# A decode step of two attention and two MLP layers with its gradients: the weighted sums over the cache taken four blocks per matmul instead of two

## The chip, the cores and the metric

The kernel runs on one core of one Trainium2 chip. The metric is the device time of one execution in microseconds (us). Before the change the median of three runs is 1138.2 us (1136.74 to 1139.24). One execution was also recorded by the hardware profiler; its span is 1136.1 us, and every figure below that is not a run time comes from that recording. The engines are named as the profile names them: PE is the matmul engine, PEld its weight loads, DVE the vector engine, ACT the scalar engine, POOL the GpSimd engine, and SP the queue that issues most transfers.

## The reference

Two rounds of attention over a key and value cache and of an MLP, for a batch of two and one new token, and then the gradients of all inputs but one. Cut to what matters here:

```python
def _A_ref(x, k_cache, v_cache, wq, wo):            # Hq=32, Hkv=4, Sk=16384, Dh=128, B=2
    q = (x @ wq).reshape(B, Sq, Hq, Dh).transpose(0, 2, 1, 3)
    k = jnp.repeat(k_cache, rep, axis=1)            # rep = 8 query heads per cache head
    v = jnp.repeat(v_cache, rep, axis=1)
    p = _softmax(jnp.einsum("bhqd,bhkd->bhqk", q, k) * (Dh ** -0.5), axis=-1)
    o = jnp.einsum("bhqk,bhkd->bhqd", p, v)
    return o.transpose(0, 2, 1, 3).reshape(B, Sq, Hq * Dh) @ wo

x = x + _A_ref(_layernorm(x), k_cache, v_cache, wq, wo)     # layer 0
x = x + _B_ref(_layernorm(x), w1, b1, w2, b2)
x = x + _A_ref(_layernorm(x), k_cache, v_cache, wq, wo)     # layer 1, same caches and weights
x = x + _B_ref(_layernorm(x), w1, b1, w2, b2)
# outputs: x and the gradients of x, both caches and the weights (jax.vjp)
```

The change concerns two sums over the 16384 cache positions: the forward output `o = p V` of each layer, and in the backward pass `dq = dS K` of layer 0 (the same sum of layer 1 is left as it is). There are 8 groups (2 batch rows x 4 cache heads), each with 8 query heads. The cache of one group is 128 blocks of 128 positions x 128 features; it is read in four chunks of 32 blocks, 1 MB each.

## The kernel before

The sums are made by the class `Acc`. One call of `quad` handles half a chunk, 16 blocks. The coefficients of two neighbouring blocks (8 heads x 2 blocks = 16 columns) are the stationary operand; the two blocks side by side (256 wide) are the moving one. Four such matmuls in a row go to four column tiles of the array (`cg` = 0, 32, 64, 96), each with its own 16 partitions of the accumulator. The accumulators of two groups lie side by side in one PSUM bank, 256 columns each. Of the 16 x 256 results of a matmul half are wanted (each head with its own block); `reduce` picks them with the selector `sel2` and adds up the four tiles.

```python
sel2 = const.tile([128, 16], F32, name="sel2")     # folds the four 32-row tiles, 16 rows each
...
e_all = pers.tile([128, G, NP, 2, 8, 2], BF16, name="e_all")   # partition, group, pair of blocks, layer, head, block
...
class Acc:
    def __init__(self, g, src, coef, finish, half=0):
        ...
        self.acc = ACCT[:, half * 256:half * 256 + 256] if half < 2 else pm_([128, 256], F32, "acc2")[:]
        zero = lambda: V.memset(self.acc, 0.0)
        ...
    def quad(self, c, q, coef=None):
        ...
            self.cv = self.pre.pop(c) if c in self.pre else kv_load(self.src, self.g, c)
        for i in range(8):
            u = c * CP + q * 8 + i
            cg = 32 * (i % 4)
            t = 2 * (q * 8 + i)
            PE.matmul(self.acc[cg:cg + 16, :], lhsT=coef(u),
                      rhs=self.cv[:, t:t + 2, :].rearrange("p t d -> p (t d)"),
                      start=False, stop=True, tile_position=(0, cg), skip_group_check=True)
    def evac(self):
        self.sb = wrk.tile([128, 2, 128], F32, name="acc_sb")
        evac_cast(self.sb[:].rearrange("p a b -> p (a b)"), self.acc, 256)
        ...
    def reduce(self):
        ...
        for t in range(2):
            PE.matmul(ps, lhsT=self.sb[:, t, :], rhs=sel2v[:, t, :], start=(t == 0), stop=(t == 1))
        self.finish(ps)
```

The forward attention works in slots, 16 per group. Each slot turns 8 key blocks by PE transposes (`emit_T`, L420), has them copied out of PSUM by ACT or DVE, and makes the 8 score matmuls of two slots before (L573). After the last score of a group come its maximum (L508), the exponentials on ACT (L537), and the 8 quads (L452), which are laid between the slots of the next group:

```python
def attn_fwd(l, q_bf, rbc, oT, groups):
    ...
    def post(g):
        max_half(g, 1)
        ...
        a = Acc(g, "V", lambda u: e_all[:, g, u, l].rearrange("p h t -> p (h t)"), finish, g % 2)
        sch.later(2, p1)
        sch.later(4, p2)
        for i in range(16):
            sch.later(5 + i // 2, lambda i=i: ex(i // 8, i % 8))
        sch.later(9, lambda: queue_acc(sch, a, range(0, 2), False))
        sch.later(13, lambda: queue_acc(sch, a, range(2, 4), True))
        ...
    while s < len(slots) + 2 or sch.busy():
        ...
        kTs[s] = emit_T(cv, b, True)                          # 8 transposes
        sch.run_slot(1 if s < len(slots) else 2)              # maybe a quad
        if 2 <= s < len(slots) + 2:
            score(s - 2)                                      # 8 score matmuls
        s += 1
```

Chunks and weights are loaded into a pool of seven 1 MB buffers (`ld`, `NLD = 7`) by SP in program order, each load as soon as a buffer comes free; the chunks of the last group stay in buffers of their own for later use.

The last pass (from about 733 us to the end) computes the gradients of both layers' caches, reads both caches again and writes both gradients; its scheduler places two quads per chunk for layer 0's dq (`dq_quad`), with coefficients `dX`, which holds both layers in the same layout as `e_all`. Most of its PE results go through four PSUM banks (`xm`) that ACT and DVE empty by copies (L161, L164).

Of the kernel before, what the change touches and what calls it, by code (L numbers as in the profile page):

```python
# [10 lines left out]
F32 = mybir.dt.float32  # L11
I32 = mybir.dt.int32
# [11 lines left out]
def kernel(  # L24
# [78 lines left out]
    def pm_(shape, dtype, name):  # L103
        return ps_sm.tile(shape, dtype, name=name, tag="sm")
# [10 lines left out]
    V.memset(ones_bf[:], 1.0)  # L115
    neghalf = const.tile([128, 2], F32, name="neghalf")
    V.memset(neghalf[:], -0.5)
    sel2 = const.tile([128, 16], F32, name="sel2")
    V.tensor_tensor(out=sel2[:], in0=identf[:, 0:16], in1=identf[:, 32:48], op=ALU.add)
    V.tensor_tensor(out=sel2[:], in0=sel2[:], in1=identf[:, 64:80], op=ALU.add)  # L120
    V.tensor_tensor(out=sel2[:], in0=sel2[:], in1=identf[:, 96:112], op=ALU.add)
    sel2v = sel2[:].rearrange("p (h t) -> p t h", t=2)
    e_all = pers.tile([128, G, NP, 2, 8, 2], BF16, name="e_all")
    hot3 = const.tile([128, 128], BF16, name="hot3")
    m3 = const.tile([128, 1], F32, name="m3")
    V.tensor_reduce(out=m3[:], in_=identf[:, 64:128:32], axis=AX.X, op=ALU.add)
# [298 lines left out]
    class Acc:  # L425

        def __init__(self, g, src, coef, finish, half=0):
            self.g, self.src, self.coef, self.finish = g, src, coef, finish  # L430
            self.pre = {}
            self.cv = None
            self.acc = ACCT[:, half * 256:half * 256 + 256] if half < 2 else pm_([128, 256], F32, "acc2")[:]
            self.half = half
            zero = lambda: V.memset(self.acc, 0.0)
            if half in Acc.in_use:
                Acc.then[half] = zero
            else:
                zero()
            Acc.in_use.add(half)  # L440

        def quad(self, c, q, coef=None):
            coef = coef or self.coef
            if q == 0 and self.get is not None:
                self.cv = self.get(c)
            elif q == 0:
                self.cv = self.pre.pop(c) if c in self.pre else kv_load(self.src, self.g, c)
            for i in range(8):
                u = c * CP + q * 8 + i
                cg = 32 * (i % 4)  # L450
                t = 2 * (q * 8 + i)
                PE.matmul(self.acc[cg:cg + 16, :], lhsT=coef(u),  # L452
                          rhs=self.cv[:, t:t + 2, :].rearrange("p t d -> p (t d)"),
                          start=False, stop=True, tile_position=(0, cg), skip_group_check=True)

        def evac(self):
            self.sb = wrk.tile([128, 2, 128], F32, name="acc_sb")
            evac_cast(self.sb[:].rearrange("p a b -> p (a b)"), self.acc, 256)
            if self.half in Acc.then:
                Acc.then.pop(self.half)()  # L460
            else:
                Acc.in_use.remove(self.half)

        def reduce(self):
            ps = px([128, 8], F32, "o_ps")[:] if self.alloc is None else self.alloc()[:, 0:8]
            for t in range(2):
                PE.matmul(ps, lhsT=self.sb[:, t, :], rhs=sel2v[:, t, :], start=(t == 0), stop=(t == 1))
            self.finish(ps)

        alloc = get = None  # L470
# [30 lines left out]
    def attn_fwd(l, q_bf, rbc, oT, groups):  # L501
        sch = Sched()
        slots = [(g, c, b) for g in groups for c in range(NCH) for b in range(NB)]
        kTs, sc, st = {}, {}, {}

        def max_half(g, f):
            m = small.tile([128, 8], F32, name="mx%d" % f)
            V.tensor_reduce(out=m[:], in_=sc[g][f][:], axis=AX.X, op=ALU.max)  # L508
            charge("D", 0.7)
            st[g].append(m)  # L510

        def post(g):
            max_half(g, 1)
            m0, m1 = st[g]
            V.tensor_tensor(out=m0[:], in0=m0[:], in1=m1[:], op=ALU.max)
            esum = small.tile([128, 2, 8], F32, name="esum")
            negm = small.tile([128, 8], F32, name="negm")
            box = {}

            def p1():  # L520
                box["pm"] = pm_([8, 128], F32, "pm")
                PE.transpose(box["pm"][:, :], m0[:], identf[:])
                gm = small.tile([8, 1], F32, name="gm")
                V.reduce_max(out=gm[:], in_=box["pm"][:, :], axis=AX.X)
                box["dg"] = small.tile([8, 8], F32, name="dg")
                V.tensor_scalar(out=box["dg"][:], in0=identf[0:8, 0:8], scalar1=gm[:, 0:1], scalar2=None, op0=ALU.mult)
                charge("D", 0.5)

            def p2():
                pm2 = pm_([128, 8], F32, "pm2")  # L530
                PE.matmul(pm2[:], lhsT=onesf[0:8, :], rhs=box["dg"][:], start=True, stop=True)
                V.tensor_scalar(out=negm[:], in0=pm2[:], scalar1=-1.0, scalar2=None, op0=ALU.mult)  # L532
                charge("D", 0.2)

            def ex(f, h):
                half = NP // 2
                S.activation(out=e_all[:, g, f * half:(f + 1) * half, l, h, :],  # L537
                             in_=sc[g][f][:, h, :].rearrange("p (a b) -> p a b", b=2),
                             func=ACT.Exp, bias=negm[:, h:h + 1], scale=1.0, accum_out=esum[:, f, h:h + 1])
                charge("A", 0.3)  # L540

            def fin1():
                V.tensor_tensor(out=esum[:, 0, :], in0=esum[:, 0, :], in1=esum[:, 1, :], op=ALU.add)

            def fin2():
                pm3 = part_sum(esum[:, 0, :], 8, "pm3")
                V.reciprocal(out=rbc[:, g, :], in_=pm3[:])

            def finish(ps):
                V.tensor_tensor(out=oT[:, g, :], in0=ps, in1=rbc[:, g, :], op=ALU.mult)  # L550

            a = Acc(g, "V", lambda u: e_all[:, g, u, l].rearrange("p h t -> p (h t)"), finish, g % 2)
            sch.later(2, p1)
            sch.later(4, p2)
            for i in range(16):
# [3 lines that stand above are left out]
            sch.later(14, fin1)  # L559
            sch.later(15, fin2)  # L560

        def score(s):
            g, c, b = slots[s]
            if c == 0 and b == 0:
                sc[g] = {}
                st[g] = []
            kT = kTs.pop(s)
            for j in range(8):
                t = c * TC + b * 8 + j
                f = t // TH  # L570
                if t % TH == 0:
                    sc[g][f] = px([128, 8, TH], F32, "sc")
                PE.matmul(sc[g][f][:, :, t % TH], lhsT=kT[:, j, :], rhs=q_bf[:, g, :], start=True, stop=True)  # L573
            if c == NCH // 2 - 1 and b == NB - 1:
                max_half(g, 0)
            if c == NCH - 1 and b == NB - 1:
                post(g)

        cv = None
        s = 0  # L580
        while s < len(slots) + 2 or sch.busy():
            sch.s = s
            if s < len(slots):
                g, c, b = slots[s]
                if b == 0:
                    cv = kv_load("K", g, c)
                kTs[s] = emit_T(cv, b, True)
            sch.run_slot(1 if s < len(slots) else 2)
            if 2 <= s < len(slots) + 2:
                score(s - 2)  # L590
            s += 1
# [733 lines left out]
    def open_dq(g):  # L1325
        def finish(ps):
            V.tensor_scalar(out=dq0[:, g, :], in0=ps, scalar1=QSCALE, scalar2=None, op0=ALU.mult)
            ready.append(g)
            if len(ready) % 2 == 0:
                quarter(g % HKV)  # L1330
        accs[g] = Acc(g, "K", None, finish, order.index(g) % 2)
        accs[g].alloc = mx
        accs[g].get = lambda c: (held_tiles["K%d" % c] if g == G - 1 else get("K", g, c))[:].rearrange(
            "p (t d) -> p t d", d=128)

    def dq_quad(i, q):
        g, c = chunks[i]
        accs[g].coef = lambda u: dX[i][:, u - c * CP, 0].rearrange("p h t -> p (h t)")
        accs[g].quad(c, q)
        if q == 1:  # L1340
            if g == G - 1:
                by_read.append(held_tiles["K%d" % c])
            else:
                done("K", g, c)
# [199 lines left out]
```

## Time and profile before

| stage | time in the span, us | mean granted PE clock | DMA, GB/s | PE busy, us |
|---|---|---|---|---|
| start, q of layer 0 | 0 to 28 | 1.00 | 371 | 11.15 |
| wo and MLP of layer 0, q of layer 1 | 190 to 271 | 0.67 | 375 | 50.95 |
| wo and MLP of layer 1, first gradients | 422 to 502 | 0.78 | 381 | 61.47 |
| attention backward of layer 1 | 502 to 662 | 0.93 | 386 | 139.56 |
| weight gradients' paths, MLP of layer 0 | 662 to 733 | 0.98 | 355 | 65.51 |
| end of the last pass | 1108 to 1136 | 0.77 | 288 | 17.95 |

The two forward attentions (28 to 190 and 271 to 422) and the body of the last pass (733 to 1108) are the stages that the change touches; their rows are shown further below. The table is the busy time of each engine cut by stage. "Busy" of PE is the time in which at least one matmul is recorded as under way, including the time for which a matmul stands in the pipeline, so a busy PE is not a PE at its peak. The clock is the share of full speed that the hardware granted. Over the whole span 449.24 MB move, at a mean of 395 GB/s; the best slices of the page show some 424 GB/s. PE is busy for 83% of the span, DVE for 56%, ACT for 50%.

### The profile page before, as it was taken

What the parts mean: (1) busy time and instruction counts of PE and PEld (TensorE: products, weight loads), DVE (VectorE), ACT (ScalarE), POOL (GpSimd) and SP (SyncE); (2) the same over time, 40 slices, a digit from 0 to 9 for tenths busy, and PEclk for the clock granted to TensorE, in tenths of its full rate; (3) what the DMA queues carried; (4) which work ended last, traced back from release to release, by engine and by line L of the source; (5) the groups of instructions that cost most, each with busy time, mean ns of one, the idle gap of its engine ahead of it and who ended that gap; (6) DMA issues with size and microseconds to landing.
All of it is one profiled execution on the core that took longest, in us unless ns stands there. A gap on an engine that the chain in (4) does not pass through costs nothing.

```text
span 1136.1 us, 38923 instructions
## 1 busy us (share of the span) xinstructions
PE 945.3 (83%) x17087; PEld 715.0 (63%) x17087; DVE 637.6 (56%) x1391; ACT 567.5 (50%) x1414; POOL 70.1 (6%) x124
## 2 busy tenths in 40 slices
PE   4978796487879885899998699988898897898896
PEld 3867675487767665898876588855555454455452
DVE  1545442133545432444746454778788767787776
ACT  0544342022535340344554344767787756686674
POOL 0000000000000000000000000022111111111210
PEclk9988976596998976899998899999999978898987
DMA  9999999998999989999999999998999999999997
GB/s 371 424 424 424 424 425 412 405 379 354 423 426 424 423 320 422 392 350 393 380 422 418 359 371 336 364 367 311 394 418 423 423 419 423 424 412 421 422 402 288
DMA packets 91962, 449.24 MB, mean 395 GB/s; under 512 B 7302, under 2 KB 7302, under 8 KB 54672
## 3 DMA queue, kind: packets, MB, share of 16 engines
q1 hardware_dynamic: 74448, 354.46, 77.4%
q0 software_dynamic: 17344, 92.29, 19.7%
q8 instruction: 133, 2.18, 0.7%
q14 instruction: 37, 0.30, 0.1%
HBM read 348.14 MB, written 98.58 MB: 393 GB/s over the span
## 4 chain that ended last, share of the span: by engine, by line
PE 50%; DMA 31%; DVE 10%; issue 4%; ACT 3%; POOL 0%; DVEq 0%; POOLq 0%; ACTq 0%; SPq 0%
DMA kv_V<-in_A_v_cache_dram 13%; PE tp L420 10%; PE wtp L270 5%; DMA kv_K<-in_A_k_cache_dram 5%; PE tpm L1451 4%; PE acc_all L452 4%; PE xm L1260 4%; DMA wt<-in_A_wo_dram 3%; DMA out_dram<-keepK 3%; DMA keepK<-in_A_v_cache_dram 3%; PE sc L573 3%; PE turn L322 3%; PE xm L1174 3%; PE dp L1313 2%; DMA out_dram<-keepxV 2%
## 5 line engine op out<-in xcount | busy, mean ns | idle before, releaser
L153 ACT COPY kT<-tp 128x512 int32<-128x512 int32 x209 | 122.8, 587 | 256.7 <-PE tp L420 247.9
L156 DVE COPY kT<-tp 128x1024 bf16<-128x1024 bf16 x159 | 108.8, 691 | 110.0 <-PE tp L420 99.1
L420 PE MATMUL tp<-ident,kv_K 128*128 128x128 bf16 x1728 | 140.3, 228 | 4.5 <-DMA kv_K<-in_A_k_cache_dram 4.5
L420 PEld LDWEIGHTS <-kv_K 128*128 128x128 bf16 x1728 | 106.3, 102 | 5.4 <-DMA kv_K<-in_A_k_cache_dram 5.3
L164 DVE CAST big<-xm 128x512 bf16<-128x512 f32 x133 | 86.4, 685 | 16.2 <-PE xm L1260 11.2
L161 ACT CAST big<-xm 128x512 bf16<-128x512 f32 x151 | 82.2, 595 | 23.2 <-PE xm L1260 13.0
L573 PEld LDWEIGHTS <-kT 128*128 128x128 bf16 x2048 | 75.9, 98 | 27.3 <-issue 21.0
L573 PE MATMUL sc<-qT_bf,kT 128*128 128x8 bf16 x2048 | 91.7, 171 | 0.3 <-issue 0.3
L161 ACT CAST keepV<-xm 128x512 bf16<-128x512 f32 (+1 forms) x137 | 75.1, 594 | 28.5 <-PE xm L1260 16.6
L420 PE MATMUL tp<-ident,kv_V 128*128 128x128 bf16 x864 | 71.5, 231 | 11.5 <-DMA kv_V<-in_A_v_cache_dram 10.6
L270 PE MATMUL wtp<-ident,wt 128*128 128x128 bf16 x928 | 75.9, 229 | 4.3 <-issue 2.9
L537 ACT ACTIVATE e_all<-sc,negm 128x64 bf16<-128x64 f32 x256 | 77.2, 345 | 1.1 <-DVE negm L532 1.0
L164 DVE CAST keepV<-xm 128x512 bf16<-128x512 f32 (+1 forms) x101 | 66.1, 685 | 18.6 <-PE xm L1260 12.3
L306 PEld LDWEIGHTS <-wt 128*128 128x128 bf16 x1696 | 48.8, 103 | 42.9 <-issue 15.2
L452 PE MATMUL acc_all<-kv_V,e_all 128*16 128x256 bf16 x864 | 46.2, 294 | 29.7 <-DMA kv_V<-in_A_v_cache_dram 16.7
L156 DVE COPY wT<-wtp 128x1024 bf16<-128x1024 bf16 (+1 forms) x64 | 41.1, 645 | 47.7 <-PE wtp L270 43.9
L153 ACT COPY wT<-wtp 128x512 int32<-128x512 int32 (+1 forms) x60 | 34.1, 568 | 64.2 <-PE wtp L270 55.8
L420 PEld LDWEIGHTS <-kv_V 128*128 128x128 bf16 x864 | 56.7, 103 | 13.3 <-DMA kv_V<-in_A_v_cache_dram 11.3
L270 PEld LDWEIGHTS <-wt 128*128 128x128 bf16 x928 | 58.1, 102 | 5.0 <-issue 3.7
L537 ACT ACTIVATION_READ_ACCUMULATOR e_all<-sc,negm 128x1 f32 x256 | 60.1, 235 | 0.0
L161 ACT CAST keepK<-xm 128x512 bf16<-128x512 f32 x98 | 52.9, 596 | 13.5 <-PE xm L1260 7.6
L1313 PE MATMUL dp<-wdo,kT 128*128 128x64 bf16 x896 | 52.2, 205 | 0.0
(369 smaller groups left out, 1750.5 us busy)
## 6 DMA issues: line engine op xcount, KB each, us to landing
kv_K<-in_A_k_cache_dram SPq DMA_DIRECT2D x81, 1024.0 KB, 11.5
kv_V<-in_A_v_cache_dram SPq DMA_DIRECT2D x81, 1024.0 KB, 12.5
wt<-in_A_wo_dram SPq DMA_DIRECT2D x32, 1024.0 KB, 9.9
wt<-in_B_w_dram SPq DMA_DIRECT2D x32, 896.0 KB, 14.0
out_dram<-big POOLq DMA_DIRECT2D x26, 1024.0 KB, 19.0
out_dram<-keepV POOLq DMA_DIRECT2D x19, 1024.0 KB, 20.0
out_dram<-keepK POOLq DMA_DIRECT2D x17, 1024.0 KB, 17.8
wt<-in_A_wq_dram SPq DMA_DIRECT2D x16, 1024.0 KB, 9.0
```

The lines of the kernel that those rows point to most:

```text
L153: S.copy(out=dst.bitcast(I32), in_=src.bitcast(I32))
L156: V.tensor_copy(out=dst, in_=src)
L161: S.copy(out=dst, in_=src)
L164: V.tensor_copy(out=dst, in_=src)
L270: PE.transpose(tp[:, o, :], wv[:, j, (o0 + o) * 128:(o0 + o + 1) * 128], ident[:])
L306: PE.matmul(fps[:, jo, :].rearrange("p (a b) -> p a b", b=2), lhsT=wv[:, j, jo * 128:(jo + 1) * 128], rhs=xT_bf[:, j0 + j, :].unsqueeze(1) ...
L420: PE.transpose(tp[:, j, :], cv[:, b * 8 + j, :], ident[:])
L452: PE.matmul(self.acc[cg:cg + 16, :], lhsT=coef(u), rhs=self.cv[:, t:t + 2, :].rearrange("p t d -> p (t d)"), start=False, stop=True, tile_ ...
L537: S.activation(out=e_all[:, g, f * half:(f + 1) * half, l, h, :], in_=sc[g][f][:, h, :].rearrange("p (a b) -> p a b", b=2), func=ACT.Exp, ...
L573: PE.matmul(sc[g][f][:, :, t % TH], lhsT=kT[:, j, :], rhs=q_bf[:, g, :], start=True, stop=True)
L1260: PE.matmul(pss[k][:], lhsT=blk[p:p + 64, o + 2 * h + k // 2, :], rhs=Qm[p:p + 64, :, :].rearrange("p a b -> p (a b)"), start=True, stop=T ...
L1313: PE.matmul(dp[:, :, t:t + 4], lhsT=kT[:, j, :], rhs=wd[:, :, x:x + 4], start=(b + j == 0), stop=False)
```

## The change

The forward sums of both layers and layer 0's dq take four cache blocks per matmul. The stationary operand is the 64 coefficient columns of two neighbouring pairs of blocks, of both layers (2 pairs x 2 layers x 8 heads x 2 blocks), which lie side by side in `e_all` and `dX`; the moving operand is the four blocks, 512 wide. A quad is then 4 matmuls instead of 8. The accumulator of a group is 64 partitions of the whole bank (partitions 0 to 63 for one group, 64 to 127 for the next), and all matmuls of a group go to the same column tile. One eighth of the results is wanted; two small copies take out the two 32 x 256 pieces that hold it, and `reduce` picks the layer's rows with one of two selectors. Because the other layer's coefficients are multiplied too, the half of `e_all` that belongs to layer 1 is set to zero at the start. The purpose is fewer matmuls and weight loads: 768 matmuls and as many weight loads less, of 17087 each. The backward attention of layer 1 keeps the form with 256 columns.

```diff
+    sel_l = const.tile([128, 32], F32, name="sel_l")
...
+    sels = [sel_l[:, 16 * l:16 * l + 16].rearrange("p (h t) -> p t h", t=2) for l in range(2)]
     e_all = pers.tile([128, G, NP, 2, 8, 2], BF16, name="e_all")
+    nc.gpsimd.memset(e_all[:, :, :, 1].rearrange("p g u h t -> p (g u) (h t)").bitcast(I32), 0)
...
+            self.r = 64 * half
+            if l is not None:
+                self.acc = ACCT[self.r:self.r + 64, :]
+            else:
+                self.acc = ACCT[:, half * 256:half * 256 + 256] if half < 2 else pm_([128, 256], F32, "acc2")[:]
...
-            for i in range(8):
-                u = c * CP + q * 8 + i
-                cg = 32 * (i % 4)
-                t = 2 * (q * 8 + i)
-                PE.matmul(self.acc[cg:cg + 16, :], lhsT=coef(u),
-                          rhs=self.cv[:, t:t + 2, :].rearrange("p t d -> p (t d)"),
-                          start=False, stop=True, tile_position=(0, cg), skip_group_check=True)
+            w = 2 if self.l is None else 4
+            for i, t in enumerate(range(16 * q, 16 * q + 16, w)):
+                r = 32 * (i % 4) if self.l is None else self.r
+                PE.matmul(self.acc[r:r + 16] if self.l is None else self.acc, lhsT=coef(c * CP + t // 2),
+                          rhs=self.cv[:, t:t + w, :].rearrange("p t d -> p (t d)"),
+                          start=False, stop=True, tile_position=(0, r), skip_group_check=True)
...
+                for k in range(2):
+                    evac_cast(self.sb[self.r + 32 * k:self.r + 32 * k + 32].rearrange("p a b -> p (a b)"),
+                              self.acc[32 * k:32 * k + 32, 256 * k:256 * k + 256], 256)
...
+            p, at = (slice(0, 128), None) if self.l is None else (slice(self.r, self.r + 64), (self.r, 0))
...
-                PE.matmul(ps, lhsT=self.sb[:, t, :], rhs=sel2v[:, t, :], start=(t == 0), stop=(t == 1))
+                PE.matmul(ps, lhsT=self.sb[p, t, :], rhs=sels[self.l or 0][p, t, :], start=(t == 0), stop=(t == 1),
+                          tile_position=at)
...
-            a = Acc(g, "V", lambda u: e_all[:, g, u, l].rearrange("p h t -> p (h t)"), finish, g % 2)
+            a = Acc(g, "V", lambda u: e_all[:, g, u:u + 2].rearrange("p u l h t -> p (u l h t)"), finish, g % 2, l)
...
-        accs[g] = Acc(g, "K", None, finish, order.index(g) % 2)
+        accs[g] = Acc(g, "K", None, finish, order.index(g) % 2, 0)
...
-        accs[g].coef = lambda u: dX[i][:, u - c * CP, 0].rearrange("p h t -> p (h t)")
+        accs[g].coef = lambda u: dX[i][:, u - c * CP:u - c * CP + 2].rearrange("p u l h t -> p (u l h t)")
```

More of the change, by code (lines that the diff above doesn't have):

```diff
@@ L117 @@
     V.memset(neghalf[:], -0.5)
[L118 to L122, printed above, removed]
+    sel_l = const.tile([128, 32], F32, name="sel_l")
+    V.tensor_tensor(out=sel_l[:], in0=identf[:, 0:32], in1=identf[:, 32:64], op=ALU.add)
+    V.tensor_tensor(out=sel_l[:], in0=sel_l[:], in1=identf[:, 64:96], op=ALU.add)
+    V.tensor_tensor(out=sel_l[:], in0=sel_l[:], in1=identf[:, 96:128], op=ALU.add)
+    sels = [sel_l[:, 16 * l:16 * l + 16].rearrange("p (h t) -> p t h", t=2) for l in range(2)]
     e_all = pers.tile([128, G, NP, 2, 8, 2], BF16, name="e_all")
+    nc.gpsimd.memset(e_all[:, :, :, 1].rearrange("p g u h t -> p (g u) (h t)").bitcast(I32), 0)
     hot3 = const.tile([128, 128], BF16, name="hot3")
@@ L425, with __init__ @@
     class Acc:
-        def __init__(self, g, src, coef, finish, half=0):
-            self.g, self.src, self.coef, self.finish = g, src, coef, finish
+        def __init__(self, g, src, coef, finish, half=0, l=None):
+            self.g, self.src, self.coef, self.finish, self.half, self.l = g, src, coef, finish, half, l
             self.pre = {}
             self.cv = None
-            self.acc = ACCT[:, half * 256:half * 256 + 256] if half < 2 else pm_([128, 256], F32, "acc2")[:]
-            self.half = half
+            self.r = 64 * half
[3 more added lines that the diff above has]
+                self.acc = ACCT[:, half * 256:half * 256 + 256] if half < 2 else pm_([128, 256], F32, "acc2")[:]
             zero = lambda: V.memset(self.acc, 0.0)
@@ L447, in quad @@
                 self.cv = self.pre.pop(c) if c in self.pre else kv_load(self.src, self.g, c)
-            for i in range(8):
-                u = c * CP + q * 8 + i
-                cg = 32 * (i % 4)
-                t = 2 * (q * 8 + i)
-                PE.matmul(self.acc[cg:cg + 16, :], lhsT=coef(u),
-                          rhs=self.cv[:, t:t + 2, :].rearrange("p t d -> p (t d)"),
-                          start=False, stop=True, tile_position=(0, cg), skip_group_check=True)
+            w = 2 if self.l is None else 4
[4 more added lines that the diff above has]
+                          start=False, stop=True, tile_position=(0, r), skip_group_check=True)
         def evac(self):
             self.sb = wrk.tile([128, 2, 128], F32, name="acc_sb")
-            evac_cast(self.sb[:].rearrange("p a b -> p (a b)"), self.acc, 256)
+            if self.l is None:
+                evac_cast(self.sb[:].rearrange("p a b -> p (a b)"), self.acc, 256)
+            else:
+                for k in range(2):
+                    evac_cast(self.sb[self.r + 32 * k:self.r + 32 * k + 32].rearrange("p a b -> p (a b)"),
+                              self.acc[32 * k:32 * k + 32, 256 * k:256 * k + 256], 256)
             if self.half in Acc.then:
```

## The prediction

> **What bounds the kernel now.** I first read the page's slices and group list, then busy time by stage, then PE's waits in each forward attention, then the timeline around one quad, and last the chain at the end of layer 1's attention.
>
> The line of the changed matmul in the groups, and busy time by stage for the three stages concerned:
>
> ```profile
> L452 PE MATMUL acc_all<-kv_V,e_all 128*16 128x256 bf16 x864 | 46.2, 294 | 29.7 <-DMA kv_V<-in_A_v_cache_dram 16.7
> ...
> core 0: us, PE busy (x) PEld busy (x) DVE busy (x) ACT busy (x) POOL busy (x), PEclk, DMA share, GB/s
> 28.00:190.00 162.00, 136.99 (x2632) 112.05 (x2630) 72.77 (x159) 71.02 (x314) 0.00 (x0) 0.87 1.01 423
> 271.00:422.00 151.00, 131.22 (x2632) 108.02 (x2633) 72.36 (x161) 71.10 (x313) 0.00 (x0) 0.91 1.00 415
> 733.00:1108.00 375.00, 330.45 (x4102) 190.82 (x4099) 289.67 (x539) 270.41 (x512) 63.37 (x106) 0.91 0.99 405
> ```
>
> One matmul lasts 294 ns, yet 864 of them cover only 46.2 us, 53 ns each: they overlap. The forward attentions run with the DMA engines full (share 1.01 and 1.00, 423 and 415 GB/s), but with PE not far behind. Slices of 30 us in the last pass show 418 to 425 GB/s from 823 to 1093 us and only 377 and 310 from 733 to 793.
>
> PE's waits in layer 0's attention, then in layer 1's:
>
> ```profile
> PE acc_all L452 <- DMA kv_V<-in_A_v_cache_dram: 10.5, 8, 3.0
> PE acc_all L452 <- DVE acc_all L435: 4.7, 7, 1.3
> PE tp L420 <- DMA kv_K<-in_A_k_cache_dram: 2.9, 4, 1.4
> ...
> PE acc_all L452 <- DVE acc_all L435: 7.0, 7, 1.3
> PE acc_all L452 <- DMA kv_V<-in_A_v_cache_dram: 6.1, 6, 1.9
> PE acc_all L452 <- ACT e_all L537: 2.8, 3, 1.8
> PE tp L420 <- DMA kv_K<-in_A_k_cache_dram: 1.7, 4, 0.7
> ```
>
> In layer 1 PE waits for data only 7.8 us of 151. It waits as long for the zeroing of the next accumulator (DVE L435).
>
> PE's timeline at one quad, full clock (start, length, instruction):
>
> ```profile
> 104.36 0.40 PE L452 MATMUL acc_all<-kv_V,e_all 128*16 128x256 bf16 x8
> 104.69 0.36 PE L573 MATMUL sc<-qT_bf,kT 128*128 128x8 bf16 x8
> 104.90 0.61 PE L420 MATMUL tp<-ident,kv_K 128*128 128x128 bf16 x8
> 105.35 0.20 PE L573 MATMUL sc<-qT_bf,kT 128*128 128x8 bf16 x2
> ```
>
> From start to start: the quad takes 0.33 us, 8 scores 0.21, 8 transposes 0.44 to 0.45. The single records inside the quad start at 104.360, .364, .367, .370 and then .473, .477, .479, .484: two waves of four, about 110 ns apart. So four 256-wide matmuls on four column tiles cost the time of one.
>
> **What the Trainium skill says.** "TensorE: Matmul & The Clock Gate", Part 3 (row/col tiling), says that small-M matmuls in distinct column groups run concurrently; the waves above agree. Part 2 (Back-to-back issue gap) gives the isolated gap as N/2.4 + 2.5 ns at full clock. For N=256 that is 109 ns, as the waves show; for N=512 an estimate of 216 ns by that page. The trace agrees: where 512-wide matmuls of L1174 with the same operands follow one another without a wait, their records start 215 ns apart. "TensorEngine Tiling (Array Packing)", Key Properties, says that a change of tiling mode drains the engine. The records show something of that size: a transpose followed by the next takes 55 ns, one followed by a quad 149 (94 more); the last matmul of a quad to the next score takes 205, about 98 over its streaming. "TensorE: Matmul & The Clock Gate", Part 1, says that the clock halves after idle windows and returns under load; the mean clocks 0.87 and 0.91 fit the waits, and a PE with fewer waits should hold 1.0.
>
> **The change part by part.**
>
> *The quad.* Before: 94 entering + 2 waves x 110 + 98 leaving = 0.41 us. After: four 512-wide matmuls, all on one 64-column tile, so nothing runs beside them: 94 + 4 x 216 + 98 = 1.06 us. The difference is +0.64 us of PE per quad. What is removed (4 weight loads and 4 issues) cost nothing before: the four starts of a wave lie within 10 ns. There are 8 groups x 8 = 64 quads in each forward layer and 64 in the last pass, so +41 us of PE work in each of the three.
>
> *Forward attention, layer 1.* A group before, at full clock: 16 slots x 0.65 = 10.4, 8 quads x 0.41 = 3.3, softmax and reduce matmuls about 1.1, so 14.9 us or 119 per layer. Summing every start-to-start gap with each kind cut to its 20th percentile gives 120.6, the same. After: 161. On top stay the waits that are not for data: L435 7.0, exponentials 2.8, and about 1.7 of small ones for the reduce, and maybe 1.5 from the doubled width of the zeroing (64 x 512 for 128 x 256), together some 13 to 14. That makes 175 us where 151 stand. Data need no more than the 151, so PE becomes the bound: **+24**. The tail is in it: the chain ends this stage with quads, then the reduce, then wo, so PE's delay there is on the path:
>
> ```profile
> 419.42 0.99 PE acc_all L452 x16
> ...
> 420.92 1.03 PE o_ps L467 x4
> ...
> 422.76 1.03 PE acc_all L306 x32
> 423.80 5.53 DMA wt<-in_A_wo_dram
> ```
>
> *Forward attention, layer 0.* The same PE work, 175 us or a little more, against 162 that the data take: +13. But part comes back. With PE the slower, DMA runs ahead and fills all seven buffers with wo before attention ends. That is so already in layer 1, where the time from the reduce (421.4) to the last wo matmul (430.1) is 8.7 us; in layer 0 it is 17.2 (189.4 to 206.6), held by wo's transfers. I take 8.5 us back and keep **+5**.
>
> *Last pass.* +41 us of PE again, but from 793 to 1093 DMA is at 393 to 425 GB/s and PE has slack: by the same cut, 265 us of work in 375. I count the places where DMA isn't full. The opening has 8 quads in a row on the chain (737.8 to 742.0): 8 x 0.64 = 5. Until 793 some 8 more, half of them hidden behind the copies: 2.5. At the end (1093 to 1108) 8 quads, of which the last two come straight before the final dq: 2 to 3. Sum **+10**.
>
> *Small parts.* Zeroing half of `e_all` on POOL is 4096 words per partition; a POOL memset of 2048 bf16 elements took 1.82 us, so about 3.6 us. It starts when POOL is done with its masks, at 1.8, and POOL is next needed at 8.90: nothing. Two 32 x 256 copies for one of 128 x 256 (0.38 to 0.42 us): about 0.35 us more on engines that are half idle, 24 times: below 1 us on the path.
>
> Sum: 1138 + 24 + 5 + 10 = **1177 us**.
>
> **The rivals.** (1) *Fewer instructions win.* If weight loads or issue limited PE, half of them would help. For it: PEld is busy 63% of the span. Against it: the eight weight loads of a quad lie within 0.11 us and the waves follow at streaming pace. It would give 1130 to 1138. (2) *Hidden under DMA.* If the stages have more slack than I think, the extra PE work fills idle time: PE shows 25 us not busy in layer 0's attention and 20 in layer 1's, clocks rise from 0.87 and 0.91 towards 1.0, and DMA needs the same time. Then layer 0 costs nothing, layer 1 about 12, the last pass 3: some 1153. Against it: 161 us of bare PE work is over layer 1's 151. (3) *The last pass pays in full.* PE, DVE and ACT take turns there through four banks, and some two fifths of that stage's chain is PE. If half of the 41 us reach the end, and layer 0 gets nothing back, it is 1138 + 24 + 13 + 20 = 1195.
>
> **Range and chances.** The sign rests on one number, 1.06 against 0.41 us for a quad, of which the old part is measured. What is loose is how much DMA hides: rival 2 gives the lower end and rival 3 the upper. I take 1157 to 1195. 2% slower is 1161; I give 0.87 to slower, 0.11 to within 2%, 0.02 to faster.
>
> **What would show it.** In the changed profile a quad should take about 0.96 us from its first start to the next score, its four starts some 216 ns apart. Layer 1's attention should last about 175 us with DMA below 370 GB/s, PE's waits for kv_V near zero, and a clock near 1.0; layer 0's about 175 with wo following in 9 us. The last pass should grow by 5 to 20. I am wrong if the four matmuls overlap (starts far closer than 216 ns), if attention stays at 162 and 151 us, or if the last pass grows by most of 41.

## The result, and the profile after

The changed kernel takes 1195.7 us (median of 4 runs, 1194.58 to 1198.23) where the kernel before takes 1138.7: a ratio of 1.0496, 95% interval 1.0467 to 1.0525. The direction was foreseen, the size was not: 57 us slower instead of 39, just above the stated range of 1157 to 1195.

The stages, from the first transpose of an attention to the last reduce of it, by the start times of the matmuls in the two recorded executions (1136.1 and 1196.5 us, so 60.4 apart where the medians are 57 apart; the last pass begins with its first L1260 or L1270 matmul):

| stage | before, us | after, us | difference | predicted |
|---|---|---|---|---|
| attention forward, layer 0 | 161.7 | 183.7 | +22.0 | +13 |
| from there to the next attention | 81.9 | 73.5 | -8.4 | -8.5 |
| attention forward, layer 1 | 150.2 | 187.0 | +36.8 | +24 |
| from there to the last pass | 312.4 | 310.1 | -2.3 | 0 |
| last pass | 402.1 | 414.4 | +12.3 | +10 |

The group line of the changed matmul on the page, then from the answer on its line its weight loads and its matmuls (duration ns min/median/max, first and last start):

```profile
L455 PE MATMUL acc_all<-kv_V,e_all 128*64 128x512 bf16 x432 | 116.0, 392 | 21.2 <-DVE acc_all L439 19.7
```

```profile
L455 PEld LDWEIGHTS <-e_all x512: 106/110/178, 48.1 to 470.0; 128*64 128x64 bf16 x171
L455 PE MATMUL acc_all<-kv_V,e_all x432: 376/379/636, 48.1 to 457.6; 128*64 128x512 bf16 x144
```

Half as many matmuls now cover 116.0 us instead of 46.2: 269 ns each instead of 53. And the idle time before them is no longer ended by a transfer (kv_V, 16.7 us) but by the zeroing of the accumulator on DVE (19.7 us).

PE's timeline at a quad of layer 1 (the prediction shows one of before):

```profile
343.31 1.05 PE L455 MATMUL acc_all<-kv_V,e_all 128*64 128x512 bf16 x4
344.29 0.36 PE L583 MATMUL sc<-qT_bf,kT 128*128 128x8 bf16 x8
344.51 0.61 PE L421 MATMUL tp<-ident,kv_K 128*128 128x128 bf16 x8
```

From its first start to the next score a quad takes 0.98 us, 0.33 before. The single records inside the quad start 240, 216 and 216 ns apart (medians in layer 1): one after another.

Busy time by stage, for the two attentions and for the stretch between them:

```profile
core 0: us, PE busy (x) PEld busy (x) DVE busy (x) ACT busy (x) POOL busy (x), PEclk, DMA share, GB/s
28.00:212.00 184.00, 167.24 (x2376) 119.38 (x2375) 75.36 (x164) 72.90 (x317) 0.00 (x0) 0.97 0.98 396
212.00:285.00 73.00, 49.71 (x1420) 48.18 (x1419) 19.67 (x60) 7.27 (x13) 2.06 (x3) 0.74 0.90 357
285.00:473.00 188.00, 168.91 (x2376) 120.43 (x2377) 75.57 (x165) 73.59 (x318) 0.00 (x0) 0.96 0.85 333
```

In layer 1 the DMA engines fall from 415 to 333 GB/s while PE's clock rises from 0.91 to 0.96 and PE is busy for 169 of 188 us: PE has become the bound. PE's waits in the same stage:

```profile
PE acc_all L455 <- DVE acc_all L439: 10.3, 7, 1.6
PE acc_all L455 <- ACT e_all L547: 2.5, 2, 1.9
PE o_ps L476 <- DVE acc_sb L165: 1.5, 2, 1.1
PE o_ps L476 <- ACT e_all L547: 1.3, 2, 0.7
PE o_ps L476 <- ACT acc_sb L162: 1.0, 2, 0.6
PE o_ps L476 <- DVE kT L157: 0.8, 1, 0.8
PE o_ps L476 <- ACT kT L154: 0.8, 1, 0.8
PE tp L421 <- DMA kv_K<-in_A_k_cache_dram: 0.6, 1, 0.6
```

No wait for V chunks is left, 0.6 us for K chunks. What remains are waits for DVE and ACT, the zeroing above all. In layer 0 the DMA engines stay busy (share 0.98), but PE's waits for data fall from the 13.4 us listed in the prediction to these 1.6, so there too PE sets the pace:

```profile
PE acc_all L455 <- DVE acc_all L439: 9.4, 7, 1.6
PE tp L421 <- DMA kv_K<-in_A_k_cache_dram: 1.6, 1, 1.6
```

### The profile page after: what moved, and what is told of

The parts are those of the page before. It is cut to its first block, busy times and chain, and to the rows that moved or that the text cites. A ratio compares the mean times of both kernels' runs of the same rounds, so it can differ in the third digit from the quotient of the medians.

```text
span 1196.5 us, 37422 instructions
## 1 busy us (share of the span) xinstructions
PE 1029.9 (86%) x16319; PEld 736.3 (62%) x16319; DVE 649.7 (54%) x1404; ACT 572.9 (48%) x1425; POOL 73.6 (6%) x125
## 4 chain that ended last, share of the span: by engine, by line
PE 68%; DVE 12%; DMA 11%; ACT 4%; issue 3%; POOL 0%; DVEq 0%; ACTq 0%; POOLq 0%
PE acc_all L455 16%; PE tp L421 12%; PE wtp L271 5%; PE sc L583 4%; PE xm L1270 4%; PE tpm L1461 4%; DMA kv_K<-in_A_k_cache_dram 3%; PE xm L1184 3%; PE turn L323 3%; DMA kv_V<-in_A_v_cache_dram 3%; PE dp L1323 2%; DMA keepK<-in_A_v_cache_dram 2%; PE acc_all L307 2%; DMA out_dram<-keepxV 2%; PE dp L682 2%
## 5 line engine op out<-in xcount | busy, mean ns | idle before, releaser
L157 DVE COPY kT<-tp 128x1024 bf16<-128x1024 bf16 x155 | 105.6, 690 | 147.1 <-PE tp L421 130.0
L421 PE MATMUL tp<-ident,kv_K 128*128 128x128 bf16 x1728 | 134.3, 222 | 2.2 <-DMA kv_K<-in_A_k_cache_dram 2.2
L455 PE MATMUL acc_all<-kv_V,e_all 128*64 128x512 bf16 x432 | 116.0, 392 | 21.2 <-DVE acc_all L439 19.7
L421 PEld LDWEIGHTS <-kv_K 128*128 128x128 bf16 x1728 | 101.7, 99 | 2.4 <-DMA kv_K<-in_A_k_cache_dram 2.4
L165 DVE CAST big<-xm 128x512 bf16<-128x512 f32 x127 | 82.5, 684 | 17.0 <-PE xm L1270 9.7
L455 PEld LDWEIGHTS <-e_all 128*64 128x64 bf16 x512 | 49.7, 113 | 67.2 <-issue 26.7
L162 ACT CAST keepV<-xm 128x512 bf16<-128x512 f32 (+1 forms) x134 | 72.2, 589 | 37.8 <-PE xm L1270 19.3
L165 DVE CAST keepV<-xm 128x512 bf16<-128x512 f32 (+1 forms) x104 | 67.6, 684 | 22.2 <-PE xm L1184 13.4
L421 PE MATMUL tp<-ident,kv_V 128*128 128x128 bf16 x864 | 69.7, 226 | 11.5 <-DMA kv_V<-in_A_v_cache_dram 10.3
L165 DVE CAST keepK<-xm 128x512 bf16<-128x512 f32 x76 | 49.1, 683 | 10.9 <-PE xm L1184 6.4
```

Source lines behind the costliest of these rows:

```text
L157: V.tensor_copy(out=dst, in_=src)
L162: S.copy(out=dst, in_=src)
L165: V.tensor_copy(out=dst, in_=src)
L421: PE.transpose(tp[:, j, :], cv[:, b * 8 + j, :], ident[:])
L455: PE.matmul(self.acc[r:r + 16] if self.l is None else self.acc, lhsT=coef(c * CP + t // 2), rhs=self.cv[:, t:t + w, :].rearrange("p t d -> ...
```

## The experiments

All runs were compared with the kernel before on the same chip (medians 1139.6 us for e1 to e4, 1140.0 for e5 to e8). The changed kernel's 1195.7 us come from its own comparison, with 1138.7 for the kernel before, so a difference to it, or between the two series, carries an uncertainty of about 1 us more. Theory A is the prediction's: the four matmuls of a quad run one after another, PE becomes the bound of the forward attentions, and the last pass is mostly hidden. What had to be found is where the other 18 us come from.

**One part alone.** First the forward sums alone in the new form, then layer 0's dq alone.

```diff
 e1: forward new, dq as before
-        accs[g] = Acc(g, "K", None, finish, order.index(g) % 2, 0)
+        accs[g] = Acc(g, "K", None, finish, order.index(g) % 2)
-        ... dX[i][:, u - c * CP:u - c * CP + 2].rearrange("p u l h t -> p (u l h t)")
+        ... dX[i][:, u - c * CP, 0].rearrange("p h t -> p (h t)")
 e2: dq new, forward as before
-            a = Acc(g, "V", lambda u: e_all[:, g, u:u + 2].rearrange("p u l h t -> p (u l h t)"), finish, g % 2, l)
+            a = Acc(g, "V", lambda u: e_all[:, g, u, l].rearrange("p h t -> p (h t)"), finish, g % 2)
```

> The forward sums of both layers in the new form, layer 0's dq in the old. Theory A (the four 512-wide matmuls of a quad run one after another on one column tile, PE becomes the bound of the two forward attentions, and the last pass adds only what the DMA engines don't hide): the last pass falls back to about 402 us, the forward attentions stay at 184 and 187 us, the time is 1181 to 1188. Theory B (the last pass, with its own 64 quads, carries a third of the loss or more): below 1176.

Measured: 1185.0 us, ratio 1.0388 (1.0370 to 1.0405); attentions of 182.6 and 186.1 us, a last pass of 405.5, 3 more than expected (the recorded execution lies 3.5 us above this median).

> Only layer 0's dq in the new form, the forward sums as before. Theory A: forward attentions of 162 and 151 us, a last pass 8 to 14 us longer than before, 1146 to 1153 in all. Theory B: 1158 or more.

Measured: 1152.8 us, ratio 1.0111 (1.0096 to 1.0126); attentions of 160.0 and 151.4 us, a last pass of 416.9, which is 14.8 longer than before and a little over what was expected. The parts add up: 45 and 13 make 58, the whole change 57. So theory B falls: more than three quarters of the loss come from the forward sums, which have 128 of the 192 quads.

**Is it the common column tile?** e3 takes the zeroing out of the forward sums and of layer 0's dq (the first matmul of a group overwrites the accumulator instead, which is possible because a group now owns all columns of its 64 partitions). e4 does the same and in addition sends the matmuls of a quad to two column tiles in turn; the two partial sums are then added in the reduce, four small copies take the place of two, and all groups share one accumulator, where two served in turn. Shapes, weights and number of the quads' matmuls are those of e3.

```diff
 e3
-            zero = lambda: V.memset(self.acc, 0.0)
+            self.n = 0
+            zero = (lambda: V.memset(self.acc, 0.0)) if l is None else (lambda: None)
-                          start=False, stop=True, ...
+                          start=self.l is not None and self.n < 1, stop=True, ...
+                self.n += 1
 e4, in addition
-                self.acc = ACCT[self.r:self.r + 64, :]
+                half = self.half = 0
+                self.acc = ACCT[:, :]
-                r = 32 * (i % 4) if self.l is None else self.r
+                r = 32 * (i % 4) if self.l is None else 64 * (i % 2)
+                          start=self.l is not None and self.n < 2, ...
```

> The changed kernel, but a group's first matmul overwrites its accumulator, so that no zeroing by DVE is waited for. Theory A with the waits added in full (in a stage that PE bounds, each wait of PE is on the path): the 19.7 us of waits for the zeroing go, each forward attention gets 8 to 10 us shorter, 1174 to 1181 in all. Rival: the wait only hides another one (exponentials, copies), and the time falls by less than 8, to 1188 or more.

Measured: 1172.9 us, ratio 1.0293 (1.0261 to 1.0325); attentions of 173.2 and 173.7 us. The gain is 22.8 us, more than the 19.7 that the waits are listed with and more than expected. A second look at the same kernel:

> A second look at e3, beside the others on this chip: 1169 to 1178.

Measured: 1173.5 us (its name is that of a variant that was not run).

> As e3, with the matmuls of a quad going in turn to two column tiles (partitions 0 to 63 and 64 to 127), same shapes and weights. Theory A: the matmuls run in pairs, a quad takes 0.62 instead of 1.06 us from the PE stream, the forward attentions are bound by DMA again (160 to 166 and 150 to 156 us), 1137 to 1150 in all. Rival C (the 64-column weights, at 107 ns against 85, or the width itself set the pace): the quads stay near 1.0 us and the time within 5 us of e3.

Measured: 1153.4 us, ratio 1.0128 (1.0096 to 1.0159); attentions of 164.1 and 160.0 us. PE's timeline at one quad:

```profile
342.17 0.62 PE L456 MATMUL acc_all<-kv_V,e_all 128*64 128x512 bf16 x4
342.73 0.36 PE L585 MATMUL sc<-qT_bf,kT 128*128 128x8 bf16 x8
```

0.56 us instead of 0.98; the records start at 342.172, .175, .412, .415, in two pairs. The weight loads have the same duration as in e3 (106 to 110 ns). So rival C falls: for the length of a quad, the column tile alone sets the difference. The gain over e3 is 19.5 us, not the 23 or more that were expected, and the times hold the other edits of e4 too: layer 1's attention stays at 160.0, where 150 to 156 were expected, and of the 9.1 us that layer 0's attention gains, 5.1 are lost again in the stretch after it (74.5 us in e3, 79.6 here). In layer 1 PE now waits for the reduce (the `o_ps` lines), 12.9 us in all; its longest waits there:

```profile
PE o_ps L478 <- DVE acc_sb L165: 4.5, 3, 1.9
PE o_ps L478 <- ACT e_all L549: 3.8, 2, 1.9
PE acc_all L456 <- ACT e_all L549: 2.4, 2, 1.9
PE o_ps L478 <- ACT kT L154: 1.8, 1, 1.8
```

**The same wait in both kernels.** The zeroing is queued on DVE behind the group's maximum, which waits for the group's last score; a quad of the group before then waits for the zeroing, though it adds to the other accumulator (why it waits for this one is not shown). Both kernels got the same edit: the accumulator is opened (and zeroed) some three slots earlier.

```diff
+            if c == NCH - 1 and b == 0:
+                opened[g] = Acc(g, "V", <coefficients>, None, g % 2 <, l>)
...
-            a = Acc(g, "V", <coefficients>, finish, g % 2 <, l>)
+            a = opened.pop(g)
+            a.finish = finish
```

> The kernel before, with the zeroing of a forward accumulator issued some three slots earlier, ahead of the maximum that DVE has to wait for. Theory A (a wait of PE costs its length only where PE is the bound; before, DMA is): the 4.7 and 7.0 us of PE's waits for the zeroing go, the time stays within 4 us of before. Rival D (these waits cost their length in either kernel): 8 to 12 us faster than before.

Measured: 1136.9 us, ratio 0.9972 (0.9956 to 0.9988), 3 us faster than before. PE's waits in layer 1's attention (before they are shown in the prediction):

```profile
PE acc_all L452 <- DMA kv_V<-in_A_v_cache_dram: 9.6, 9, 1.8
PE acc_all L452 <- ACT e_all L538: 3.1, 3, 2.1
PE tp L420 <- DMA kv_K<-in_A_k_cache_dram: 2.2, 4, 0.7
```

The 7.0 us for the zeroing are gone, and the waits for data have grown from 7.8 to 11.8: more than half of what one wait gave, the other took.

> The same edit in the changed kernel, nothing else. Theory A: PE's 9.4 and 10.3 us of waits for the zeroing go and the time falls by 16 to 24 us, about as with e3, to 1172 to 1180. Rival: with the zeroing still there the wait only moves, and less than 8 us are gained.

Measured: 1173.6 us, ratio 1.0291 (1.0267 to 1.0315), 22 us less than the changed kernel. Attentions of 173.3 and 174.3 us, as with e3. In layer 1 no wait for the zeroing is listed any more; the first line is now

```profile
PE acc_all L455 <- ACT e_all L548: 2.5, 2, 1.9
```

One edit, of the same waits, is worth 3 us in the kernel where they are listed with 11.7 us in both attentions, and 22 in the one where they are listed with 19.7. Rival D falls, and so does the rival that the wait would only move.

**The reduce's wait.** e8 gives e4's reduce four slots instead of two.

```diff
-                sc_.later(2, a.reduce)
+                sc_.later(2 if a.l is None else 4, a.reduce)
```

> As e4, with the reduce of a forward group four slots after its copies instead of two. In e4 PE waits some 10 to 15 us per layer for the reduce (the four small copies and the exponentials ahead of them). Theory A: these waits go, the second attention falls from 160 to 150 to 154 us, the time to 1138 to 1148. Rival: what is left of the longer quad keeps PE at the bound, 1150 or more.

Measured: 1164.1 us, ratio 1.0211 (1.0189 to 1.0232): slower than e4 by about 10 us. It lies in the rival's "1150 or more", but a loss against e4 was expected by neither side. In the two recorded executions it is all in layer 1's attention (171.3 us against 160.0). The waits there, up to 440 us:

```profile
PE acc_all L456 <- ACT e_all L549: 14.1, 8, 2.4
PE acc_all L456 <- DMA kv_V<-in_A_v_cache_dram: 1.4, 2, 0.8
PE o_ps L478 <- ACT acc_sb L162: 1.2, 1, 1.2
```

The reduce hardly waits any more (the last one, after 440 us, still 1.9 us), but the first quad of each group waits for its exponentials in its stead (8 times, up to 2.4 us). So in e4 the reduce stood in a place where PE had to wait anyway. And the clock of the stage fell, e4 first:

```profile
271.00:432.00 161.00, 143.69 (x2376) 108.20 (x2377) 76.11 (x167) 75.96 (x325) 0.00 (x0) 0.93 0.95 389
```

```profile
271.00:440.00 169.00, 150.79 (x2372) 112.99 (x2372) 74.28 (x159) 75.95 (x325) 0.00 (x0) 0.87 0.92 370
```

With the same matmuls PE is busy 7 us longer. By the records of the granted clock, layer 1's attention runs at half clock for 45.0 us in e8 and for 22.0 in e4. As an estimate, 23.0 us more at half clock can cost up to 11.5, and the stage lost 11.3. Why the clock fell is not shown: no run changed the clock alone, and e4 too has single waits of up to 1.9 us.

## Why the prediction was right or wrong

**The quad, right.** 1.06 us was predicted, 0.96 of it from the first start to the next score; 0.98 was measured, and with the 94 ns of entering 1.08. That the common column tile is the cause is shown by e4.

**PE becomes the bound in layer 1's attention, right.** DMA fell to 333 GB/s (below 370 was named), waits for V chunks vanished, the clock rose (0.96; "near 1.0" was named). The pair e5 and e6 shows it by experiment: PE's waits count where PE is the bound.

**What layer 0 gets back, right.** 8.4 us against 8.5: the last wo matmul comes 10.1 us after the reduce (211.5 to 221.6), 17.2 before. The 9 us named for it were about met.

**The last pass, right in sum.** +12.3 against +10 (and +14.8 in e2, +3.4 in e1, where its own quads are as before). By the reduce of the second group it is 8.8 us behind (82.6 us after its start instead of 73.8), against 7.5 predicted for that stretch. After that the delay goes up and down: 14.7 at the fourth reduce, 7.7 at the fifth, 9.3 at the seventh, 12.3 at the end. So the shares that the sum gave to single places are shown for the first stretch only.

**The zeroing of half of `e_all`, right.** It took 3.51 us on POOL (3.6 estimated) and delayed nothing on the path: the first transpose of layer 0's attention starts at 27.8 us in both executions.

**The step that failed: "On top stay the waits that are not for data", together "some 13 to 14".** This term gave the 175 us of both attentions, where 184 and 187 were measured. By the sum of the start-to-start gaps, cut as in the prediction, layer 1's attention has 164 us of bare PE work (161 predicted; 1.3 of the 3 are the 0.02 us by which a quad is longer than predicted) and 23 us above it. The parts:
- The zeroing: 8.5 predicted, 10.3 listed as idle, and 12.7 to 13.3 gained when it goes (187.0 to 174.3 in e6, to 173.7 in e3). I carried the old waits over and added 1.5 for the seven of them. But like for like each gap in the PE stream grew by about 0.32 us: one zeroing takes 485 ns instead of 272, and DVE begins it some 0.1 us later. From the start of PE's last instruction to the start of its next quad, where 0.15 us is usual without a wait, it takes 1.4 us instead of 1.06 where DVE is free for the maximum, and 1.8 instead of 1.4 to 1.5 where a key copy stands ahead of it on DVE. That is so in four of the seven cases in layer 1, before in two (the seventh case, at the tail, went from 1.48 to 1.8 too).

  The 2 to 3 us by which the gain exceeds the listed 10.3 fit the clock: e6 has 11.0 us at half clock in this attention, the changed kernel 15.9. In layer 0 the zeroing is worth 10.5 (183.7 to 173.2) against the same 8.5 in the sum.

  One zeroing in the kernel before:

```profile
318.22 0.27 DVE L435 MEMSET acc_all<- 128x256 f32 x1
```

  DVE's timeline of one case, the changed kernel:

```profile
338.67 0.69 DVE L157 COPY kT<-tp 128x1024 bf16<-128x1024 bf16 x1 [1.53 <-PE tp L421]
339.27 0.68 DVE L518 TENSOR_REDUCE mx<-sc 128x8 f32<-128x512 f32 x1
339.99 0.17 DVE L525 TENSOR_TENSOR mx<-mx,mx 128x8 f32<-128x8 f32 x1
340.31 0.48 DVE L439 MEMSET acc_all<- 64x512 f32 x1 [0.15 <-issue]
```

  PE began its last transpose at 339.06 and its next quad at 340.85, with 1.57 us idle between them:

```profile
340.85 1.02 PE L455 MATMUL acc_all<-kv_V,e_all 128*64 128x512 bf16 x4 [1.57 <-DVE acc_all L439]
```
- The reduce: 1.7 predicted, 5.4 listed. The two small copies take 0.36 to 0.43 us each, no less than the one wide copy before (0.37 to 0.42), and most start one after the other, so the second is ready some 0.4 us later. I had called them "below 1 us on the path". That they are the whole of the 5.4 is not shown: part of it is listed as waits for exponentials and key copies.
- The exponentials: 2.8 predicted, 2.5 listed.
- The rest, about 5 us of the 23 by the listed waits, is not divided further. The sum had nothing for a lowered clock, and 15.9 us of layer 1's attention still ran at half clock, which can cost up to 8 us by the same estimate as above.

So the mechanism was right and the term of waits was mis-sized: 23 us instead of 13 to 14 in layer 1, and 20 in layer 0 (184.6 us of gaps, cut in the same way, 164.7 of them bare work). The mistake in kind was to list waits from a kernel in which they cost little (3 us gained in e5) and to carry them, nearly unchanged, into one in which they lie on the path (22 us in e6).

**The rivals.** Rival 1 (fewer instructions win) and rival 2 (hidden under DMA) did not happen. Rival 3 came nearest in number (1195) for another reason: it put the surplus into the last pass and into layer 0's return, both of which were as predicted.

## What to carry to other kernels

Count matmuls that run at the same time on different column tiles as one: replacing two waves of four 256-wide matmuls by four 512-wide ones on one tile halved the instructions and took a quad's time in the PE stream from 0.41 to 1.08 us, 2.6 times as long. When a change moves the bound from DMA to an engine, every wait of that engine has to be sized again in the new kernel (what stands ahead in the queue, how long the operation is after the change), since the old profile shows it where it cost nothing. The best kernel of this study is the old one with its accumulators zeroed earlier (e5), by 0.3%.

## What was unexpected

Moving a reduce two slots later, which took away the waits that it was meant to take away, made the kernel about 10 us slower (e8): the wait moved to the first quad of the next group, and the time at half clock in layer 1's attention went from 22.0 to 45.0 us. The Trainium skill, "TensorE: Matmul & The Clock Gate", Part 1, says that the clock halves after an idle window of some 3.4 us; the waits listed in that stage are 2.4 us at most, so either shorter gaps suffice when they come with other thin stretches, or something else lowers it. No run here tells which.

Within a quad on one tile the first two starts lie 240 ns apart and the others 216, both in the changed kernel and, between the pairs, in e4 (342.172 to 342.412). The prediction's 216 for all four was short by these 24 ns; why the first is longer is open.
